# Sigmoid attention and a gated layer on one core: attention of all batches first, and the gated layer's products in 2x2x2 blocks with seven products in place of eight

## The chip, the core and the metric

The kernel runs on one core of a Trainium2 chip. Five engines work on their own instruction queues, each in order: TensorE (PE in the profile; its weight loads are PEld), VectorE (DVE), ScalarE (ACT), GpSimd (POOL) and SyncE (SP, which here only starts transfers). They wait for each other by semaphores. The metric is the device time of one execution in microseconds (us), the median of several runs; 675.48 us before the change. Where a reader sees "a product" below, it is a run of matmuls that sum into one PSUM bank.

## The reference, cut to what matters

```python
batch, n_heads, seq, head_dim = (4, 12, 448, 64)
d_model, d_ff = 768, 1536
scores = scale * np.matmul(q, k.transpose(0, 1, 3, 2)) - np.log(S)
attn = 1.0 / (1.0 + np.exp(-scores))            # a sigmoid, no sum over keys
attn_out = np.matmul(attn, v)
x = attn_out.transpose(0, 2, 1, 3).reshape(B * S, H * D)      # 1792 x 768
rms = np.sqrt(np.mean(x * x, axis=-1, keepdims=True) + 1e-06)
xn = x / rms * rms_g
g, val = xn @ w_gate, xn @ w_val                # 768 -> 1536, twice
out = (g * (1.0 / (1.0 + np.exp(-g))) * val) @ w_out          # 1536 -> 768
```

All in float32; the weights arrive as the bits of float64.

## The kernel before

A float32 operand of a product is held as two fp16 parts, hi and lo, and a product is hi·hi + hi·lo + lo·hi: three matmuls for each 128 rows of the contraction. A part is made by ScalarE (hi, a copy with a scale, `hi_of`) and VectorE (lo, `lo_of`). Weights are first put together as float32 from the two words of a float64 by three VectorE instructions on 768 columns (lines 349, 352, 353), then split.

Attention runs by pairs of heads, 24 pairs in all, six to a batch; a pair has four groups of keys (g = 0 to 3; the last, `MID`, has half the work). For each pair VectorE splits q and k (`qk_hi`, `qk_lo`, two pairs ahead), a transfer transposes them into T, VectorE swaps halves of T (`k_swap`, one pair ahead) and copies the shared slot of v (`v_mid`). `scores(i, g)` is four matmuls and a sigmoid on ScalarE; `av(i, g)` multiplies with v. For 13 of the pairs (`exact`: batches 0 and 1 and the last pair) the products with v are float32's own; for the other 11 the sigmoid's result and v are split, and the products are three fp16 matmuls.

The program is written out in order (`manual_schedule`). It takes two batches at a time: attention of batches 0 and 1, the gated layer of both for each slice of 128 columns of its weights (`ffn_in`, 18 matmuls of 448 columns for one batch and one of gate and value, 1728 in all), then the output layer of these two batches (`out_steps`) woven into the attention of batches 2 and 3, then the gated layer and the output layer of those. The gated layer's weights are so loaded and split twice, once for each two batches. In attention scores and products with v alternate group by group: scores of one group, then the product of the group `LAG` = 3 behind.

The rms norm of a batch (`norm`) is a list of parts: a matmul that sums squares over the features (`squares`), small VectorE steps (mean, guess, three Newton steps, `spread` to a diagonal), a matmul that spreads the factor to all rows (`rows`, called rinv in the profile), and six scalings with their hi and lo. The parts are drawn from the list `later`, with waits in between by the table `WAITS`.

Of the kernel before, what the change touches and what calls it, by code (L numbers as in the profile page):

```python
# [15 lines left out]
# Powers of two that keep both fp16 parts of a float32 operand in fp16's range.  # L16
SQ = 2.0**6
SA = 2.0**15
SX = 2.0**6
SW = 2.0**6  # L20
# [4 lines left out]
def attention_then_swiglu(  # L25
# [25 lines left out]
    NCC = DM // P  # L51
    NFC = DFF // P
    HALF = DM // 2
    NTOK = 2 * S // P
    TB = S // 4
# [3 lines left out]
    ld_p = ctx.enter_context(tc.tile_pool(name="ld", bufs=4))  # L59
    nat_p = ctx.enter_context(tc.tile_pool(name="nat", bufs=2))  # L60
    v_p = ctx.enter_context(tc.tile_pool(name="v", bufs=3))
    t_p = ctx.enter_context(tc.tile_pool(name="t", bufs=3))
    s_p = ctx.enter_context(tc.tile_pool(name="s", bufs=3))
    a_p = ctx.enter_context(tc.tile_pool(name="a", bufs=4))
    x_p = ctx.enter_context(tc.tile_pool(name="x", bufs=2))
    r_p = ctx.enter_context(tc.tile_pool(name="r", bufs=2))
    f_p = ctx.enter_context(tc.tile_pool(name="f", bufs=5))
    win_p = ctx.enter_context(tc.tile_pool(name="win", bufs=2))
    h_p = ctx.enter_context(tc.tile_pool(name="h", bufs=1))
    o_p = ctx.enter_context(tc.tile_pool(name="o", bufs=2))  # L70
# [11 lines left out]
    ATT = 0.82  # L82
    OUT_STEP = 4
    WARM = 20
    WAITS = ((9, 2, 1, 2, 1), (0, 1, 0, 1, 2), (8, 2, 0, 3, 3), (5, 2, 0, 4, 2))
# [5 lines left out]
    wo = const.tile([P, 2, NFC, DM], F16, name="wo")  # L91
    v3 = [const.tile([P, 2, 2 * D], F16, name=f"v3_{i}") for i in range(3)]
# [4 lines left out]
    def hi_of(engine, hi, f, scale):  # L97
        if engine is nc.scalar:
            nc.scalar.activation(hi, f, AF.Copy, scale=scale)  # L99
        else:  # L100
            nc.vector.tensor_scalar(hi, f, scale, None, ALU.mult)  # L101

    def lo_of(lo, f, hi, scale):
        nc.vector.scalar_tensor_tensor(lo, f, scale, hi, ALU.mult, ALU.subtract)  # L104

    lo_q = []

    def flush(keep):
# [4 lines left out]
    pairs = [(b, hp) for b in range(B) for hp in range(NPAIR)]  # L113
    ld, nat, vt, qkT, at, pav, xt, acc = ({} for _ in range(8))
# [5 lines left out]
    def load_qk(i, queue=nc.scalar):  # L120
        t = ld_p.tile([P, 2 * DM], F32, tag="ld", name="qkv")[:, : 3 * NSLOT * D]
        t = ld[i] = t.rearrange("p (t c d) -> p t c d", t=3, c=NSLOT)
        queue.dma_start(t[:, 0], rows_of(q, i, "(p c) d -> p c d"))  # L123
        queue.dma_start(t[:, 1], rows_of(k, i, "(c p) d -> p c d"))

    def load_v(i):
        vt[i] = v_p.tile([P, 2, NSLOT, D], F16, tag="nv", name="nv")
        if exact(i):
            vt[i] = vt[i].rearrange("p l c d -> p (l c d)").bitcast(F32).rearrange("p (c d) -> p c d", d=D)
        nc.sync.dma_start(vt[i] if exact(i) else ld[i][:, 2], rows_of(v, i, "(c p) d -> p c d"))  # L130

    # Parts of the rows of q and k: transposed they are [qh|ql] and [kh|kl], with [kl|kh] from the second;
    # a head's tokens are its queries in the order of every NSLOT-th one.
    def qk_hi(i):
        n = nat[i] = nat_p.tile([P, 2, NSLOT, 2, D], F16, tag="n", name="n")
        hi_of(nc.vector, n[:, :, :, 0], ld[i][:, 0:2], SQ)

    def qk_lo(i):
        n = nat[i]
        lo_of(n[:, :, :, 1], ld[i][:, 0:2], n[:, :, :, 0], SQ)  # L140

    def transpose(i):
        T = qkT[i] = t_p.tile([P, 3, NSLOT, P], F16, tag="T", name="T")
# [12 lines left out]

    def v_hi(i):
        if not exact(i):
            hi_of(nc.vector, vt[i][:, 0], ld[i][:, 2], SQ)

    def v_lo(i):
        if not exact(i):
            lo_of(vt[i][:, 1], ld[i][:, 2], vt[i][:, 0], SQ)

    def v_mid(i):
        """The slot that two heads share: once with either one's rows, over zeros."""
        for j in range(2):
            rows = slice(64 * j, 64 * j + 64)
            if exact(i):
                nc.vector.tensor_copy(v3[i % 3].bitcast(F32)[rows, j], vt[i][rows, MID])  # L170
            else:
                nc.vector.tensor_copy(v3[i % 3].rearrange("p j (l d) -> p j l d", l=2)[rows, j], vt[i][rows, :, MID])

    split_q = []

    def split_a(keep):
        while len(split_q) > keep:
            sg, a = split_q.pop(0)
            hi_of(nc.scalar, a[:, 0], sg, SA)
            lo_of(a[:, 1], sg, a[:, 0], SA)  # L180

    def scores(i, g):
        """Sigmoid of the scores, keys on partitions: 128 keys of either head, or 64 of each."""
        T = qkT[i]
        n = 1 if g == MID else 2
        ps = ps_s.tile([P, 2, 512], F32, tag="sc", name="sc")
# [20 lines left out]
        if g == MID:  # L207
            del qkT[i]
# [398 lines left out]
```

## Time and profile before

| | |
|---|---|
| median of 3 runs (lowest, highest) | 675.48 us (675.33, 676.51) |
| span of the profiled execution, first to last instruction | 672.7 us |
| PE busy in the span | 654.9 us, 97% |
| PE weight loads | 329.4 us, 49% |
| DVE busy | 420.7 us, 63% |
| ACT busy | 260.9 us, 39% |

The profile lists one execution, so its own time is the span and about 2.8 us that lie outside the first and last instruction, if it took as long as the median. A group of instructions is a line, an engine, an operation and a tile; "x36" counts them. In the views that go in order of time the first number is the start in us from the span's start, the second the length; a bracket at the end is the idle time of that engine just before, and what ended it. "PEclk" is the granted clock of TensorE as a share of 2.4 GHz; between its two levels, 1.00 and 0.50, a value is a mean over the stretch. A float32 matmul shows as two records.

### The profile page before, as it was taken

To read this page: it belongs to the slowest core of one execution; us is meant where nothing else is said; L and a number is where in the kernel's file an instruction comes from. 1 tells how busy PE (TensorE), PEld (TensorE's weight loads), DVE (VectorE), ACT (ScalarE), POOL (GpSimd) and SP (SyncE) were. 2 spreads that over 40 slices of the span, in tenths; PEclk is the share of its full clock that TensorE was granted. 3 is DMA by queue.
4 is the path that set the end of the run, shared out by engine and by line. 5 is a ranking of instruction groups with operands and counts; after the bars stand their busy time and mean duration, and the time that the engine had idled before them with its cause. 6 is when DMAs were issued, how large, how long until landed. Compare 5 with 4: busy or idle time off the path is not lost.

```text
span 672.7 us, 9121 instructions
## 1 busy us (share of the span) xinstructions
PE 654.9 (97%) x3672; PEld 329.4 (49%) x3672; DVE 420.7 (63%) x695; ACT 260.9 (39%) x392; POOL 0.7 (0%) x6
## 2 busy tenths in 40 slices
PE   7999999999999999999999999899999999999995
PEld 5233345555555554444454455355555555566663
DVE  4586786998888897778968637477576655100000
ACT  2666743333332335676766743123222222100000
POOL 0000000000000000000000000000000000000000
PEclk8999999999999999999999999899999999999998
DMA  9999730555455545788774002534323410011111
GB/s 195 237 251 208 198 107 1 188 189 188 147 188 183 187 130 110 174 135 175 144 145 85 25 22 89 182 111 154 111 94 120 128 36 0 1 32 34 33 35 33
DMA packets 134953, 80.80 MB, mean 120 GB/s; under 512 B 89856, under 2 KB 133376, under 8 KB 134912
## 3 DMA queue, kind: packets, MB, share of 16 engines
q1 hardware_dynamic: 115904, 71.97, 41.3%
q10 hardware_dynamic: 19008, 8.26, 5.3%
q8 instruction: 28, 0.46, 0.3%
q14 instruction: 13, 0.11, 0.0%
HBM read 63.70 MB, written 5.51 MB: 103 GB/s over the span
## 4 chain that ended last, share of the span: by engine, by line
PE 93%; DMA 4%; DVE 1%; ACT 0%; SPq 0%; issue 0%; ACTq 0%; DVEq 0%
PE h L368 47%; PE o L396 25%; PE av L226 10%; PE sc L195 10%; DMA T<-n 3%; DMA raw<-in_moe_w_val_dram 1%; DMA qkv<-in_k_dram 1%; PE ssq L262 1%; PE rinv L289 0%; DVE T L151 0%; ACT o L406 0%; DVE win L104 0%; DVE wf L353 0%; DVE wf L352 0%; SPq L123 0%
## 5 line engine op out<-in xcount | busy, mean ns | idle before, releaser
L368 PE MATMUL h<-x,win 128*128 128x448 f16 x1728 | 329.3, 354 | 2.8 <-DVE win L101 2.4
L368 PEld LDWEIGHTS <-win 128*128 128x128 f16 x1728 | 169.1, 98 | 162.5 <-DVE win L101 2.8
L396 PE MATMUL o<-wo,h 128*128 128x384 f16 x1008 | 170.3, 327 | 0.0
L396 PEld LDWEIGHTS <-h 128*128 128x128 f16 x1008 | 96.7, 98 | 72.2 <-issue 9.2
L195 PE MATMUL sc<-T 128*128 128x448 f16 (+1 forms) x384 | 81.9, 360 | 4.8 <-DMA T<-n 3.3
L99 ACT ACTIVATE win<-wf 128x768 f16<-128x768 f32 x40 | 33.7, 844 | 102.2 <-DVE wf L353 102.2
L382 DVE SCALAR_TENSOR_TENSOR hf<-h,hf 128x448 f32<-128x448 f32 x48 | 29.8, 620 | 52.5 <-PE h L368 52.5
L226 PE MATMUL av<-a,nv 128*64 128x448 f16 (+1 forms) x354 | 61.9, 446 | 0.0
L202 ACT ACTIVATE a<-sc,bias_s 128x896 f32<-128x896 f32 (+1 forms) x52 | 47.4, 915 | 31.6 <-PE sc L195 31.6
L195 PEld LDWEIGHTS <-T 128*128 128x128 f16 (+1 forms) x384 | 29.0, 102 | 61.7 <-issue 39.3
L353 DVE SCALAR_TENSOR_TENSOR wf<-raw,wf 128x768 uint32<-128x768 uint32 x56 | 53.6, 957 | 1.4
L104 DVE SCALAR_TENSOR_TENSOR win<-wf,win 128x768 f16<-128x768 f32 x48 | 45.9, 957 | 13.6 <-ACT win L99 13.4
L383 ACT ACTIVATE h<-hf 128x448 f16<-128x448 f32 x48 | 27.3, 570 | 67.8 <-DVE hf L382 67.8
L352 DVE SCALAR_TENSOR_TENSOR wf<-raw,wf 128x768 uint32<-128x768 uint32 x56 | 53.3, 952 | 0.1
L104 DVE SCALAR_TENSOR_TENSOR a<-sg,a 128x896 f16<-128x896 f32 (+1 forms) x44 | 42.8, 974 | 16.3 <-ACT a L99 15.8
L202 ACT ACTIVATE sg<-sc,bias_s 128x896 f32<-128x896 f32 (+1 forms) x44 | 40.0, 912 | 27.6 <-PE sc L195 21.0
L406 ACT ACTIVATE o<-o 128x384 f32<-128x384 f32 x28 | 13.7, 488 | 88.3 <-PE o L396 87.1
L99 ACT ACTIVATE a<-sg 128x896 f16<-128x896 f32 (+1 forms) x44 | 37.4, 850 | 0.0
L377 ACT ACTIVATE hf<-h 128x448 f32<-128x448 f32 x48 | 25.5, 531 | 23.2 <-PE h L368 23.2
L385 DVE TENSOR_TENSOR h<-hf,h 128x448 f16<-128x448 f32 x48 | 29.9, 622 | 6.9 <-ACT h L383 6.9
L349 DVE TENSOR_SCALAR wf<-raw 128x768 uint32<-128x768 uint32 x56 | 30.9, 553 | 3.7 <-DMA raw<-in_moe_w_val_dram 3.6
L104 DVE SCALAR_TENSOR_TENSOR n<-qkv,n 128x896 f16<-128x896 f32 x24 | 26.1, 1088 | 0.3
(50 smaller groups left out, 260.8 us busy)
## 6 DMA issues: line engine op xcount, KB each, us to landing
raw<-in_moe_w_gate_dram SPq DMA_DIRECT2D x22, 768.0 KB
raw<-in_moe_w_val_dram SPq DMA_DIRECT2D x22, 768.0 KB
raw<-in_moe_w_out_dram SPq DMA_DIRECT2D x12, 768.0 KB
out_dram<-o SPq DMA_DIRECT2D x24, 192.0 KB
qkv<-in_q_dram ACTq DMA_DIRECT2D x18, 224.0 KB
qkv<-in_k_dram ACTq DMA_DIRECT2D x18, 224.0 KB
nv<-in_v_dram SPq DMA_DIRECT2D x13, 224.0 KB
qkv<-in_v_dram SPq DMA_DIRECT2D x11, 224.0 KB
```

What stands on the lines that cost most here:

```text
L99: nc.scalar.activation(hi, f, AF.Copy, scale=scale)
L104: nc.vector.scalar_tensor_tensor(lo, f, scale, hi, ALU.mult, ALU.subtract)
L195: nc.tensor.matmul(o, m, r, start=(w == 0), stop=(w == 1))
L202: nc.scalar.activation(sg, ps[:, :n, :S], AF.Sigmoid, bias=bias_s, scale=1.0 / (math.sqrt(D) * SQ * SQ))
L226: nc.tensor.matmul(ps[64 * j : 64 * j + 64, :S], w, m, start=(g == 0 and n == 0), stop=(g == MID and n == len(parts) - 1),)
L349: lambda: nc.vector.tensor_scalar(b, r[:, :, 1], 3, 0x3FFFFFF8, ALU.logical_shift_left, ALU.bitwise_and),
L352: lambda: stt(b, r[:, :, 0], 29, b, ALU.logical_shift_right, ALU.bitwise_or),
L353: lambda: stt(b, r[:, :, 1], 0xC0000000, b, ALU.bitwise_and, ALU.bitwise_or),
L368: nc.tensor.matmul(ps[:, :S], w[:, g, l, c * P : c * P + P], xn(b, c, r), start=(c == 0 and n == 0), stop=(c == NCC - 1 and n == 2),)
L382: nc.vector.scalar_tensor_tensor(f, ps[:, :S], SH / (SX * SW), hold.pop(b), ALU.mult, ALU.mult)
L385: lambda: nc.vector.tensor_tensor(h[:, 1, fc, cols], f, h[:, 0, fc, cols], ALU.subtract)
L396: nc.tensor.matmul(ps[:, :HALF], h[:, l, c, t * P : t * P + P], wo[:, r, c, cols], start=(c == 0 and n == 0), stop=(c == NFC - 1 and n == 2),)
```

## The change

Attention of all four batches comes first, by the float32 products with v for all 24 pairs. Groups go by two: scores of two groups, then the products with v of the two groups before. The norms of batches 0, 1 and 2 and the splitting of the first two slices of the weights are drawn from `later` during attention, by a budget: each part has a cost, and a half step allows 0.72 (`SHARE`). `squares` now follows the last product of its batch where the list is empty.

Then comes the gated layer for all batches. Two batches (rows of x), two halves of the features and gate/value make a 2x2x2 block; `quad` computes such a block with seven products of half the contraction (9 matmuls each, 63 in all) where eight would be 72. For that the norm of the odd batch makes four sums and differences of x (1344 columns each), and `split_w` four of the weights (384 columns each); seven operands are split into hi and lo instead of four. Each slice of the weights is loaded and split once. The results are put together by VectorE: three additions of 448 columns, one of 896, two products and one lo of 896 to a quad. There are 24 quads of 63 matmuls, 1512.

The output layer comes last, for all batches; its first eight results are summed side by side in all eight PSUM banks, slice by slice of w_out, while the later slices are split. SBUF is divided by hand: buffers of attention, of the gated layer and of the output layer share the same places.

```diff
-    Two batches at a time: attention of their heads, the gated layer of both for each slice of
-    its weights, and the layer that follows together with the next two batches' attention."""
...
-    LAG = 3
-    W_FROM = (13, 17)
-    W_WAIT = 10
-    LATER_IN = 8
-    LATER_OUT = 5
...
-    WAITS = ((9, 2, 1, 2, 1), (0, 1, 0, 1, 2), (8, 2, 0, 3, 3), (5, 2, 0, 4, 2))
+    W_FROM = 40
+    SHARE = 0.72
...
+        def scale(k):
+            tt(x[:, k], x[:, k], ps[1][:, :S].unsqueeze(1).to_broadcast([P, NK, S]), ALU.mult)
+
+        def hi(slot, f):
+            nc.scalar.activation(xc[n, slot][:, 0], f, AF.Copy)
+
+        def lo(slot, f):
+            tt(xc[n, slot][:, 1], f, xc[n, slot][:, 0], ALU.subtract)
+
+        parts = [(squares, 0.2), (wait, 0.7), (mean, 0.2), (guess, 0.5)] + [(newton, 0.5)] * 3
+        parts += [(spread, 1.1), (rows, 0.2), (wait, 0.7)]
...
+        queue = [(s1, x[:, 0], x[:, 1], ALU.add, 3), (s2, s1, x0[:, 0], ALU.subtract, 4)]
+        queue += [(s4, x0[:, 1], s2, ALU.subtract, 6), (x[:, 0], x0[:, 0], x[:, 0], ALU.subtract, 5)]
...
+    def split_w(fc):
...
+        for o, f0, f1 in ((4, 2, 0), (2, 3, 2), (5, 3, 4), (6, 1, 5)):
+            first.append((lambda o=o, f0=f0, f1=f1: tt(wf[:, o], wf[:, f0], wf[:, f1], ALU.subtract), 0.6))
+
+        def hi(s):
+            nc.scalar.activation(t[:, 0, s], wf[:, s], AF.Copy, scale=SW)
+
+        def lo(s):
+            stt(t[:, 1, s], wf[:, s], SW, t[:, 0, s], ALU.mult, ALU.subtract)
+
+        cuts = [slice(0, 2), slice(2, 4), slice(4, 7)]
+        second.append((lambda: [hi(s) for s in cuts], 0.0))
+        second += [(lambda s=s: lo(s), 1.1) for s in cuts]
...
+    def quad(fc, n, fill):
+
+        y = y_b[(fc * NQ + n) % 2]
+        pa, pc = bank("ca"), banks("cc")
+        run_behind()
+        product(pa[:, :S], fc, n, 0, 0)
+        nc.scalar.activation(u_b, pa[:, :S], AF.Copy)
+        run_behind()
+        fill(0)
+        pb = bank("cb")
+        product(pb[:, :S], fc, n, 4, 5)
+        tt(u_b, u_b, pb[:, :S], ALU.add)
+        run_behind()
+        product(pc[:, 1, :S], fc, n, 5, 2)
+        tt(c_b, u_b, pc[:, 1, :S], ALU.add)
+        fill(1)
+        product(pc[:, 0, :S], fc, n, 3, 4)
+        tt(c_b, c_b, pc[:, 0, :S], ALU.add)
+        fill(2)
+        product(pa[:, :S], fc, n, 1, 1, True)
+        nc.scalar.activation(g_b, pa[:, :S], AF.Silu, scale=UNIT)
+        fill(3)
+        product(pc[:, 1, :S], fc, n, 2, 6, True)
+        fill(4)
+        product(pc[:, 0, :S], fc, n, 6, 3, True)
+
+        def sums():
+            tt(y, pc[:, :, :S], u_b.unsqueeze(1).to_broadcast([P, 2, S]), ALU.add)
+            nc.scalar.activation(y[:, 1], y[:, 1], AF.Silu, scale=UNIT)
...
+    def run_later(share):
+        credit[0] = min(credit[0] + share, 1.6)
+        while later and credit[0] > 0:
+            part, cost = later.pop(0)
+            part()
+            credit[0] -= cost
...
+        for n in range(0, len(todo) + 2, 2):
+            for i, g in todo[n : n + 2]:
+                scores(i, g)
+                for part in FILL[g]:
+                    part(i)
+                run_later(SHARE)
+            for i, g in todo[max(n - 2, 0) : n]:
+                av(i, g)
+                b, hp = pairs[i]
+                if hp == NPAIR - 1 and g == MID:
+                    later.extend(norm(b))
+                run_later(SHARE)
+            if n == W_FROM:
+                load_w(0)
+            if n == W_FROM + 16:
+                for fc in range(2):
+                    first, second = split_w(fc)
+                    later.extend(first + second)
...
+        for c in range(NFC):
+            for (t, e), ps in zip(first, pss):
+                out_part(ps, t, e, c)
+            if c + 3 < NFC:
+                if c + 6 < NFC:
+                    load_o(c + 6)
+                for x in sum(split_o(c + 3), []):
+                    x()
```

VectorE's queue during attention, one pair before the change while the first weights are split (`qkv`, `n`, `T`: q and k as loaded, split, transposed; `wf`, `win`: weights as float32 and split):

```order
L242 TENSOR_TENSOR acc<-acc,sq 128x448
L349 TENSOR_SCALAR wf<-h 128x768
L352 SCALAR_TENSOR_TENSOR wf<-h,wf 128x768
L101 TENSOR_SCALAR n<-qkv 128x14x64
L353 SCALAR_TENSOR_TENSOR wf<-h,wf 128x768
L101 TENSOR_SCALAR win<-wf 128x768
L104 SCALAR_TENSOR_TENSOR n<-qkv,n 128x14x64
L150 COPY T<-T 64x896
L151 COPY T<-T 64x896
```

The same queue now, at the pairs that the splitting of the first weights falls on (`xc` holds q, k and T there, `wr` the weights):

```order
L177 TENSOR_SCALAR xc<-xc 128x14x64
L328 SCALAR_TENSOR_TENSOR wr<-wr 128x768
L181 SCALAR_TENSOR_TENSOR xc<-xc 128x14x64
L191 COPY xc<-xc 64x896
L192 COPY xc<-xc 64x896
L355 TENSOR_TENSOR wr<-wr 128x384 x3
L198 COPY room<-room 64x64 x2
L355 TENSOR_TENSOR wr<-wr 128x384
L361 SCALAR_TENSOR_TENSOR wr<-wr 128x768 x2
L177 TENSOR_SCALAR xc<-xc 128x14x64
L361 SCALAR_TENSOR_TENSOR wr<-wr 128x1152
L181 SCALAR_TENSOR_TENSOR xc<-xc 128x14x64
```

Between one pair's `qk_lo` and `k_swap` and the next pair's stood at most one weight's splitting, with ten half steps of pause before each; now parts of the weights and of the norms stand there in every pair from the end of batch 1 to the last but one.

TensorE's queue at the first batch's sum of squares, before (`sc`, `av`, `ssq`: scores, products with v, sum of squares):

```order
L226 MATMUL av<-a,v_0_105 64x448 x2
L195 LDWEIGHTS T
L195 MATMUL sc<-T 64x448
...
L262 MATMUL ssq<-ones,acc 112x1 x4
L226 MATMUL av<-a,nv 64x448 x2
```

and now (`rinv`: the matmul that spreads the norm's factor):

```order
L252 MATMUL ssq<-ones,room 112x1 x4
L213 LDWEIGHTS xc
L213 MATMUL sc<-xc 128x448
...
L213 MATMUL sc<-xc 64x448
L227 MATMUL av<-room 64x448 x4
L279 MATMUL rinv<-room,ones 128x448
```

The sum of squares came one group of scores behind the batch's last product; it now comes right behind that product, and rinv two groups of scores and two of products later.

VectorE's queue in the gated layer, before, about one product of a gate and one of a value for one batch:

```order
L382 SCALAR_TENSOR_TENSOR hf<-h,hf 128x448
L349 TENSOR_SCALAR wf<-raw 128x768
L385 TENSOR_TENSOR h<-hf,h 128x448
L352 SCALAR_TENSOR_TENSOR wf<-raw,wf 128x768
L353 SCALAR_TENSOR_TENSOR wf<-raw,wf 128x768
L349 TENSOR_SCALAR wf<-raw 128x768
L104 SCALAR_TENSOR_TENSOR win<-wf,win 128x768
```

and now, one quad with the end of the quad before it (`cb`, `cc`: PSUM banks of the products):

```order
L355 TENSOR_TENSOR wr<-wr 128x384 x4
L418 TENSOR_TENSOR room<-cc,room 128x896
L422 SCALAR_TENSOR_TENSOR room<-room 128x448
L423 SCALAR_TENSOR_TENSOR room<-room 128x448
L402 TENSOR_TENSOR room<-room,cb 128x448
L427 TENSOR_TENSOR room<-room 128x896
L405 TENSOR_TENSOR room<-room,cc 128x448
L408 TENSOR_TENSOR room<-room,cc 128x448
L361 SCALAR_TENSOR_TENSOR wr<-wr 128x768 x2
L361 SCALAR_TENSOR_TENSOR wr<-wr 128x1152
```

What VectorE does for one result grew, and two of TensorE's seven products (lines 413 and 415, into `cc`) wait until it has read the bank that they add to (lines 405 and 408).

## Rows read from the trace of the kernel before

**Rows 1.** The page's first part: the span, and each engine's busy time, share and instructions.

```profile
span 672.7 us, 9121 instructions
PE 654.9 (97%) x3672; PEld 329.4 (49%) x3672; DVE 420.7 (63%) x695; ACT 260.9 (39%) x392; POOL 0.7 (0%) x6
```

**Rows 2.** Busy time of each engine by stage of the program: stretch, its length, then PE, PEld, DVE, ACT, POOL, granted clock, share of the DMA engines, GB/s. The stages: attention of batches 0 and 1, their gated layer, their output layer with attention of batches 2 and 3, the gated layer of these, and after the last output product.

```profile
11.20:94.00 82.80, 80.96 (x402) 27.27 (x403) 57.56 (x122) 57.03 (x79) 0.00 (x0) 0.98 1.01 217
94.00:260.40 166.40, 165.38 (x873) 85.13 (x871) 144.83 (x215) 53.00 (x86) 0.00 (x0) 1.00 0.47 147
260.40:414.60 154.20, 154.20 (x992) 76.75 (x991) 110.17 (x207) 98.01 (x140) 0.00 (x0) 1.00 0.53 107
414.60:583.00 168.40, 165.60 (x867) 84.86 (x866) 102.05 (x140) 44.14 (x72) 0.00 (x0) 0.99 0.31 100
665.00:672.70 7.70, 0.00 (x0) 0.00 (x0) 0.00 (x0) 0.40 (x1) 0.00 (x0) 0.64 0.09 29
```

**Rows 3.** The chain of work that ended last, followed back from the end: shares by engine.

```profile
PE 93%; DMA 4%; DVE 1%; ACT 0%; SPq 0%; issue 0%; ACTq 0%; DVEq 0%
```

**Rows 4.** The costliest group, the gated layer's matmuls, from the table of groups (count, busy us, mean ns of one record), and two pieces of the chain in order of time: the last output layer, and ScalarE's copy of its last result.

```profile
L368 PE MATMUL h<-x,win 128*128 128x448 f16 x1728 | 329.3, 354 | 2.8 <-DVE win L101 2.4
```
```profile
582.92 81.91 PE o L396 x504
...
664.91 0.49 ACT o L406
```

**Rows 5.** Pieces of the chain in attention of batches 0 and 1: a group's scores (four matmuls), a group's product with v (two matmuls, four records), the same place of the next pair, and the four last groups of products with v in a row.

```profile
42.74 0.86 PE sc L195 x4
43.60 0.90 PE av L226 x4
...
49.17 0.86 PE sc L195 x4
...
88.75 3.06 PE av L226 x16
```

**Rows 6.** TensorE in order of time in the same attention, one group of scores seen in two windows that end after its second and its fourth matmul.

```profile
57.29 0.55 PE L195 MATMUL sc<-T 128*128 128x448 f16 x2
```
```profile
57.29 0.93 PE L195 MATMUL sc<-T 128*128 128x448 f16 x4
```

**Rows 7.** The end of batch 1 and its norm in order of time: square on ScalarE, sum on VectorE, the sum of squares on TensorE (with TensorE's idle time before it in brackets), the first and the last of VectorE's small steps, and rinv.

```profile
91.83 0.54 ACT L239 ACTIVATE sq<-av 128x448 f32<-128x448 f32 x1 [1.86 <-PE av L226]
...
92.41 0.62 DVE L242 TENSOR_TENSOR acc<-acc,sq 128x448 f32<-128x448 f32 x1 [0.28 <-ACT sq L239]
...
93.09 0.95 PE L262 MATMUL ssq<-ones,acc 128*112 128x1 f32 x8 [1.33 <-DVE acc L242]
...
96.99 0.15 DVE L267 TENSOR_SCALAR m<-ssq 112x4 f32<-112x4 f32 x1
...
99.36 0.84 DVE L283 TENSOR_SCALAR diag<-ident,y 112x112 f32<-112x112 f32 x4
...
100.70 0.92 PE L289 MATMUL rinv<-diag,ones 112*128 112x448 f32 x2
```

**Rows 8.** VectorE's instructions by form from the table of groups (count | busy us, mean ns of one): joining of weights, splits and sums of 448, 768 and 896 columns, the swap and the copy of v's shared slot; and ScalarE's copy of 768 columns.

```profile
L353 DVE SCALAR_TENSOR_TENSOR wf<-raw,wf 128x768 uint32<-128x768 uint32 x56 | 53.6, 957 | 1.4
L349 DVE TENSOR_SCALAR wf<-raw 128x768 uint32<-128x768 uint32 x56 | 30.9, 553 | 3.7 <-DMA raw<-in_moe_w_val_dram 3.6
L385 DVE TENSOR_TENSOR h<-hf,h 128x448 f16<-128x448 f32 x48 | 29.9, 622 | 6.9 <-ACT h L383 6.9
L104 DVE SCALAR_TENSOR_TENSOR n<-qkv,n 128x896 f16<-128x896 f32 x24 | 26.1, 1088 | 0.3
L101 DVE TENSOR_SCALAR n<-qkv 128x896 f16<-128x896 f32 x24 | 15.0, 623 | 14.2 <-DMA qkv<-in_k_dram 14.1
L150 DVE COPY T<-T 64x896 f16<-64x896 f16 x24 | 9.3, 387 | 7.7 <-DMA T<-n 7.1
L170 DVE COPY v<-nv 64x64 f32<-64x64 f32 x26 | 4.9, 187 | 0.6
...
L99 ACT ACTIVATE win<-wf 128x768 f16<-128x768 f32 x40 | 33.7, 844 | 102.2 <-DVE wf L353 102.2
```

**Rows 9.** Two transfers as pieces of the chain: weights, 768 KB with other such loads beside them, and a pair's transpose.

```profile
415.95 8.16 DMA raw<-in_moe_w_val_dram
```
```profile
6.19 4.15 DMA T<-n
```

**Rows 10.** Four stretches as in rows 2: the busiest ten us of VectorE in attention, a stretch with TensorE's wait at batch 1's norm, and two with the longest idle times of TensorE; behind them, in order of time, the matmuls that ended these two idle times.

```profile
30.00:40.00 10.00, 9.99 (x49) 3.09 (x50) 9.66 (x17) 6.38 (x8) 0.00 (x0) 1.00 1.19 250
90.00:100.00 10.00, 8.67 (x51) 4.42 (x48) 9.13 (x26) 2.80 (x4) 0.00 (x0) 1.00 0.00 0
420.00:440.00 20.00, 17.20 (x83) 8.15 (x81) 8.66 (x13) 2.79 (x6) 0.00 (x0) 0.91 0.49 162
...
10.00:20.00 10.00, 9.15 (x37) 3.07 (x38) 5.95 (x12) 5.48 (x6) 0.00 (x0) 0.83 1.10 203
```
```profile
10.39 0.36 PE L195 MATMUL sc<-T 128*128 128x448 f16 x1 [2.77 <-DMA T<-n]
```
```profile
427.33 0.55 PE L368 MATMUL h<-x,win 128*128 128x448 f16 x2 [2.36 <-DVE win L101]
```

More of the change, by code (lines that the diff above doesn't have):

```diff
@@ new lines, in hi @@
+        def hi(slot, f):
[4 more added lines that the diff above has]
+        parts += [(spread, 1.1), (rows, 0.2), (wait, 0.7)]
+        if not odd:
+            for s in range(2):
+                parts += [
+                    (lambda s=s: scale(s), 1.6),
+                    (lambda s=s: hi(s, x[:, s]), 0.0),
+                    (wait, 0.7),
+                    (lambda s=s: lo(s, x[:, s]), 1.6),
+                ]
+            return parts
@@ L345, in split_w, with wait, to_f32 @@
+        return parts + [(wait, 0.7), (lambda a=behind: lo(*a), 1.6)]
+    def wait():
+        pass
+    def to_f32(f, r):
         b = f.bitcast(U32)
-        hi, lo = dest(u)
-        stt = nc.vector.scalar_tensor_tensor
         return [
@@ new lines, in attention_then_swiglu, with run_behind, product @@
+    PARTS = ((0, 0), (0, 1), (1, 0))
+    UNIT = 1.0 / (SX * SW)
+    behind = []
+    def run_behind():
+        if behind:
+            behind.pop(0)()
+    def product(ps, fc, n, a, b, more=False):
+        w = win[fc % 2]
+        for c in range(NK):
+            for m, (l, r) in enumerate(PARTS):
+                nc.tensor.matmul(
+                    ps,
+                    w[:, l, b, c],
+                    xc[n, a][:, r, c],
+                    start=(not more and c == 0 and m == 0),
+                    stop=(c == NK - 1 and m == 2),
+                    skip_group_check=more,
+                )
@@ new lines, in out_part, with out_end @@
+    def out_part(ps, t, e, c):
+        for n, (l, r) in enumerate(PARTS):
+            nc.tensor.matmul(
+                ps[:, :HALF],
+                h[c, t // NTOK][:, l, t % NTOK * P : t % NTOK * P + P],
+                wo[c][:, r, e * HALF : e * HALF + HALF],
+                start=(c == 0 and n == 0),
+                stop=(c == NFC - 1 and n == 2),
+            )
+    def out_end(ps, t, e):
+        cols = slice(e * HALF, e * HALF + HALF)
+        o = o_b[(2 * t + e) % 4]
+        nc.scalar.activation(o, ps[:, :HALF], AF.Copy, scale=1.0 / (SH * SO))
+        rows = out.rearrange("(b p c) d -> b c p d", b=B, c=NSLOT)
+        for j in range(2):
+            b, c = divmod(2 * t + j, NSLOT)
+            (nc.sync, nc.scalar)[j].dma_start(rows[b, c, :, cols], o[64 * j : 64 * j + 64])
@@ new lines, in attention_then_swiglu @@
+        first = [(t, e) for t in range(4) for e in range(2)]
+        pss = []
+        for _ in range(2):
+            both = banks("o2")
+            pss += [both[:, 0], both[:, 1]]
+        while behind:
+            run_behind()
+        pss += [bank("o") for _ in range(4)]
+        for c in range(NFC):
[6 more added lines that the diff above has]
+                    x()
@@ L580 @@
+        for (t, e), ps in zip(first, pss):
+            out_end(ps, t, e)
+        for t in range(4, NQ * NTOK):
+            for e in range(2):
+                ps = bank("o")
+                for c in range(NFC):
+                    out_part(ps, t, e, c)
+                out_end(ps, t, e)
 _INS = ["q", "k", "v", "moe_w_gate", "moe_w_val", "moe_w_out", "moe_rms_g"]
```

536 lines of the change are left out of this document (205 added, 331 removed).

## Prediction

> **What bounds the kernel now.** I read the page's busy times first: TensorE is busy for 654.9 of 672.7 us, VectorE for 420.7 [rows 1]. The chain of waits agrees, 93% of it is PE [rows 3]. An average says little of a change that moves whole stages, so the windows by stage come next: in each stage but the first and the last TensorE is busy for 98 to 100% and the clock is at 0.98 to 1.00 [rows 2]. Last, is TensorE really at its peak when it is busy? The gated layer's 1728 matmuls take 329.3 us, 190.6 ns each; 448 columns at the granted 2.4 GHz are 186.7 ns. The output layer's 504 take 81.91 us, 162.5 ns each [rows 4]. So the time is the count of matmuls, and it falls only if fewer are issued and no other engine takes TensorE's place. VectorE is the one to watch: at its busiest it works 9.66 of 10 us while TensorE still does 9.99 [rows 10].
>
> **What is removed.** 216 of 1728 gated matmuls: 216 x 0.1906 = 41.2 us. The second splitting of the weights goes too, but it lay on VectorE beside a full TensorE, so by itself it gives nothing.
>
> **What TensorE gets more of.** All pairs now take the float32 products with v. Such a pair takes 49.17 - 42.74 = 6.43 us with groups in alternation [rows 5]. A three-pass pair is bounded by the third stage: 154.2 us [rows 2], less 81.9 of output layer [rows 4], over 12 pairs: 6.0 (one of these pairs is exact already). So eleven pairs lose some 0.4 to 0.5 each, about 5 us. Groups by two give part back: a matmul of scores inside a run takes (0.93 - 0.55) / 2 = 0.19 us, so four take 0.76 [rows 6], against 0.86 between products with v; a group of products takes 3.06 / 4 = 0.765 in a run, 0.90 alone [rows 5]. If half of the switches go, a pair saves about 0.25 us: **6.17 us**.
>
> **What VectorE gets in attention.** A pair needs a split of q and k (0.623 + 1.088), two swaps (0.387 each), two copies (0.187 each) and one sum (0.622): 3.5 us [rows 8], far below 6.17. In batches 0 and 1 that stays so: norm 0 is four 1344-column instructions and small steps, spread over six pairs. From batch 1's sum of squares to the end of attention, 11.75 pairs, the order of VectorE's queue holds:
> - 9 splits, 10 pairs of swaps, 12 pairs of copies and 10 sums: 15.4 + 7.8 + 4.5 + 6.2 = 33.9 us;
> - two norms: small steps 3.2 each (96.99 to 100.20) [rows 7], and 15 instructions of 1344 columns. The trace has none so wide. From 448 to 896 columns the time goes from 0.622 to 1.088 [rows 8], 1.04 ns a column, so 1.56 us each as an estimate (the bound below is the 1.088 of 896, were the wide ones cheap): 6.4 + 23.4 = 29.8;
> - two splittings of weights: joining 2 x (0.553 + 2 x 0.957), four differences of 384 columns (0.55, by the same slope), two lo of 768 (0.957) and one of 1152 (1.36) [rows 8]: 10.4 each, 20.9 in all.
>
> That is **84.5 us on VectorE against 11.75 x 6.17 = 72.5, with the norms' matmuls 75 to 77, on TensorE**. VectorE becomes the bound of this half. It can't put the work off: the queue is in order, and the parts stand between one pair's split and the next pair's swap, without which that pair's scores don't start. I add 3 us for transposes queued on SP behind 1.5 MB of weights (8.16 us a load against 4.15 for a transpose [rows 9]; bounds 0 and 8), 0.4 for rinv, and 2.7 for the last pairs, where VectorE has little left and TensorE ends alone: 90.6.
>
> **The sum**, against the profiled execution (span 672.7; the 2.8 us outside it are kept):
> - start, unchanged: 11.2.
> - batches 0 and 1, now 80.6 us (11.21 to 91.8, the start of batch 1's last square [rows 2, 7]): twelve pairs save 3.0; two more groups of scores, 1.6; norm 0 adds 2.1, a wait of 1.3 for its sum as at batch 1 today [rows 7], since `squares` no longer has a group of scores ahead of it, and 0.8 for rinv, beside 0.95 and 0.92 that it costs today as well. 81.3, to 92.5.
> - batch 1's sum: wait 1.33 and 0.95 [rows 7]: 94.8.
> - batches 2 and 3, VectorE-bound: 90.6, to 185.4; batch 3's sum 0.95: 186.4.
> - gated layer: 1512 x 0.1906 = 288.2, and 5.6 in its first quads, where batch 3's norm (3.2 of small steps, then sums) is late and rinv takes 0.92: 480.2.
> - output layer, all batches: 1008 x 0.1625 = 163.8, and 2 for the last quad's sums, which must end before their PSUM banks are taken: 646.0. Its splitting of a slice (2.46 joining, 0.844 on ScalarE, 0.957 [rows 8]) runs three slices ahead.
> - tail 7.7 to 7.8 [rows 2]: 653.8.
>
> 653.8 against 672.7 is 18.9 less; with 2.8 outside, **656.6, say 657 us**. Of the 41.2 us, 22.3 are given back, 18 of them in the half that VectorE bounds (90.6 - 72.5).
>
> **Why the gated layer costs nothing more.** A quad lasts 63 x 0.1906 = 12.0 us on TensorE. For two quads VectorE has 10.4 of weights and 2 x (5 x 0.622 for 448 columns + 2 x 1.088 for 896 [rows 8] = 5.3) for the results, 21.0 together against 24.0, 88%. The places that can stall are the sixth and seventh product (lines 413 and 415), which add to a bank that VectorE must have read. By the order it has read them at 6.2 and 7.8 us into the quad; TensorE comes there at 8.6 and 10.3. Cover is 2.4 us, and a part of the weights (at most 1.36) in the way leaves over 1 us of it. If that cover were gone, a wait would cost its length 24 times.
>
> **Rivals.**
> *B, the backlog is hidden:* wide VectorE instructions nearer the lower bound (15 x 0.47 = 7 us less) and TensorE stays the bound in attention: 13 us less, 644. For: 9.66 busy and no wait [rows 10]. Against: the slope in rows 8, and the sum must fall by over 8 us. 0.07.
> *G, the quads stall:* the PSUM banks come 0.5 us late in every quad, 24 x 0.5 = 12: 669. For: VectorE at 88%, in order, with waits on ScalarE's copies between. Against: the cover above. It is slower than before only from 0.77 us a quad. 0.13.
> *C, slower, by the clock:* in the VectorE-bound half TensorE waits for about 1.5 us in a mean pair (90.6 / 11.75 = 7.7, less 6.17), and for 3.5 in one with four wide instructions (3.5 + 4 x 1.56 = 9.7). Rows 10 have the clock at 0.83 in the ten us of an idle time of 2.77 and at 0.91 in the twenty of one of 2.36; after 1.33 us it stays at 1.00. A pair wholly at the lower level, 1.2 GHz, would take 12.3 us instead of 7.7, 4.6 more: from four of the twelve pairs the saving of 18 is gone, and with seven the time is 656.6 + 32, about 689. Against: what a low clock takes comes out of the idle time first. One drop as in 420 to 440 costs 0.09 x 20 = 1.8 us of TensorE's work, and 6.17 + 1.8 = 8.0 is only 0.3 above the mean pair; then TensorE has no idle time and the clock rises again, as it did behind both waits. 0.10.
> The Trainium skill ("TensorE: Matmul & The Clock Gate", section "HAM oscillation — how this bites in real kernels") says that a wait in each iteration can throw the clock back at each of them, so that the price is paid per iteration and not once; by that rule the time would be rival C's. Rows 10 agree that a single wait does it; no row of the kernel before shows it repeated.
> The change does do what it says: 63 matmuls a quad are in the order. What remains, 0.04, is a mixture of G and small waits, 674 to 677, no change.
>
> **How the numbers follow.** Forecast 652 to 667 (transposes 0 to 8, norm and wide instructions by their bounds): 0.66. B 0.07, G 0.13, C 0.10, the rest 0.04. 0.2%, 1.35 us, is about what a measurement can tell from no change. Faster: 0.66 + 0.07 + most of G = 0.84; within 0.2%: 0.05; slower: C and a remainder of G, 0.11. The range goes from 647, which leaves out most of B, to 672, which takes in most of G: what is outside is C, B, the rest and a little of G, 0.2.
>
> **What would show it.** Attention ends at about 186 us; from 95 to 183 VectorE is busy for over 95% and TensorE for about 80%, with its waits before scores, ended by `k_swap` on VectorE. 24 quads at 12.0 us, with no idle time before lines 413 and 415. Output layer 166 us, tail 7.8. Wrong: a granted clock well under 1.00 from 95 to 185 (C), idle times in each quad (G), or TensorE near 100% in that half (B).

## The result and the profile after

The changed kernel takes **684.27 us** (median of 4 runs, 682.68 to 685.66) against 675.4 of the kernel before: a ratio of 1.014, with a 95% interval of 1.0112 to 1.0169. It is slower, where 657 was forecast. The profiled execution has a span of 680.9 us.

The page's first part, for the span and the busy times [rows 1], and the chain's shares by engine [rows 3]:

```profile
span 680.9 us, 8362 instructions
PE 625.7 (92%) x3368; PEld 314.8 (46%) x3368; DVE 412.1 (61%) x639; ACT 242.5 (36%) x332; POOL 0.7 (0%) x6
```
```profile
PE 54%; DVE 33%; issue 5%; ACT 4%; DMA 2%; ACTq 0%; SPq 0%; DVEq 0%
```

TensorE's busy time did fall, by 29.2 us. But the span left over grew from 18 to 55 us, and a third of the chain, 1% before, now runs through VectorE. Where, the windows by stage tell (columns as in [rows 2]); the stages are attention of batches 0 and 1, of 2 and 3, the gated layer, the output layer, and what follows its last product:

```profile
11.20:92.00 80.80, 78.28 (x401) 29.23 (x401) 49.60 (x104) 56.91 (x74) 0.00 (x0) 0.98 1.00 197
92.00:190.30 98.30, 82.30 (x409) 31.36 (x406) 80.31 (x150) 66.21 (x86) 0.00 (x0) 0.95 0.69 146
190.30:509.10 318.80, 293.36 (x1517) 148.88 (x1517) 243.01 (x334) 95.25 (x133) 0.00 (x0) 0.98 0.18 57
509.10:676.90 167.80, 164.43 (x1009) 98.50 (x1007) 34.33 (x41) 22.40 (x39) 0.00 (x0) 1.00 0.21 65
676.90:680.90 4.00, 0.00 (x0) 0.00 (x0) 0.00 (x0) 0.46 (x1) 0.00 (x0) 1.00 0.19 49
```

| stretch | forecast, us | profiled, us | difference |
|---|---|---|---|
| start to batch 1's sum of squares | to 93.85 | to 93.86 | 0.0 |
| from there to the first quad | 92.55 | 96.4 | +3.9 |
| gated layer | 293.8 | 318.8 | +25.0 |
| output layer | 165.8 | 167.8 | +2.0 |
| tail | 7.8 | 4.0 | -3.8 |

The sum is 27.1, which is 680.9 less the forecast 653.8. The gated layer is the miss: of its 25.0 us, some 20 lie in the last 22 of the 24 quads and 4.8 in the first two. TensorE is busy for 293.36 us in it, and 25.4 us are idle time. (That 293.36 is close to the 293.8 forecast for the whole stage is chance: the forecast had 288.2 of gated matmuls and 5.6 of the first quads.) The table of groups says before what, for the products into `cc`:

```profile
L382 PE MATMUL cc<-xc,wr 128*128 128x448 f16 x864 | 176.8, 355 | 25.4 <-DVE room L405 25.4
```

And the instructions of one quad in order of time (idle time of the engine in brackets) say which product: the second of the two groups of nine into `cc` here is the quad's fourth product, line 407:

```profile
421.27 1.87 PE L382 MATMUL cc<-xc,wr 128*128 128x448 f16 x9
...
421.54 0.62 DVE L402 TENSOR_TENSOR room<-room,cb 128x448 f32<-128x448 f32 x1 [0.99 <-ACT room L424]
422.07 1.08 DVE L427 TENSOR_TENSOR room<-room 128x896 f16<-128x896 f32 x1
423.17 0.62 DVE L405 TENSOR_TENSOR room<-room,cc 128x448 f32<-128x448 f32 x1
423.84 1.86 PE L382 MATMUL cc<-xc,wr 128*128 128x448 f16 x9 [0.71 <-DVE room L405]
```

The third product runs into one bank of the pair; line 405 reads that bank when it ends; the fourth product goes into the other bank and yet starts only when line 405 is done. TensorE stands idle for 0.71 us here and for 0.86 to 0.93 in every other quad: 16.6 us in 21 quads. The second quad, behind batch 3's norm, waits for 6.70 us and the last for 2.11; only the first has no wait, since rinv stands there between the third and the fourth product.

```profile
502.28 1.86 PE L382 MATMUL cc<-xc,wr 128*128 128x448 f16 x9 [2.11 <-DVE room L405]
```

### The profile page after: what moved, and what is told of

Same layout as the page of the kernel before. It is cut to its first block, busy times and chain, and to the rows that moved or that the text cites. A ratio compares the mean times of both kernels' runs of the same rounds, so it can differ in the third digit from the quotient of the medians.

```text
span 680.9 us, 8362 instructions
## 1 busy us (share of the span) xinstructions
PE 625.7 (92%) x3368; PEld 314.8 (46%) x3368; DVE 412.1 (61%) x639; ACT 242.5 (36%) x332; POOL 0.7 (0%) x6
## 3 DMA queue, kind: packets, MB, share of 16 engines
q1 hardware_dynamic: 92400, 48.97, 29.2%
## 4 chain that ended last, share of the span: by engine, by line
PE 54%; DVE 33%; issue 5%; ACT 4%; DMA 2%; ACTq 0%; SPq 0%; DVEq 0%
PE o L449 24%; PE cc L382 13%; PE av L227 6%; PE sc L213 6%; PE ca L382 4%; DVE room L418 4%; DVE wr L355 3%; DVE wr L327 3%; DVE room L405 2%; DVE room L402 2%; DVE room L422 2%; DMA xc<-xc 2%; DVE wr L328 2%; DVE wr L324 2%; DVE room L423 2%
## 5 line engine op out<-in xcount | busy, mean ns | idle before, releaser
L382 PEld LDWEIGHTS <-wr 128*128 128x128 f16 x1512 | 148.5, 98 | 169.6 <-issue 35.3
L382 PE MATMUL cc<-xc,wr 128*128 128x448 f16 x864 | 176.8, 355 | 25.4 <-DVE room L405 25.4
L449 PE MATMUL o<-xc,room 128*128 128x384 f16 x798 | 133.3, 326 | 3.3 <-ACT room L460 2.4
L449 PEld LDWEIGHTS <-room 128*128 128x128 f16 x798 | 78.1, 98 | 55.2 <-issue 3.7
L215 ACT ACTIVATE room<-sc,bias_s 128x896 f32<-128x896 f32 x96 | 84.3, 916 | 48.0 <-PE sc L213 46.6
L213 PE MATMUL sc<-xc 128*128 128x448 f16 (+1 forms) x384 | 78.4, 364 | 12.3 <-ACT room L215 6.9
L227 PE MATMUL av<-room 128*64 128x448 f32 x384 | 84.3, 559 | 0.0
L460 ACT ACTIVATE room<-o 128x384 f32<-128x384 f32 x28 | 13.7, 491 | 111.3 <-PE o L449 107.5
L382 PE MATMUL ca<-xc,wr 128*128 128x448 f16 x216 | 46.0, 359 | 0.0
L382 PE MATMUL cb<-xc,wr 128*128 128x448 f16 x216 | 44.8, 352 | 0.0
L327 DVE SCALAR_TENSOR_TENSOR wr<-wr 128x768 uint32<-128x768 uint32 x31 | 29.7, 959 | 1.0
L328 DVE SCALAR_TENSOR_TENSOR wr<-wr 128x768 uint32<-128x768 uint32 x31 | 29.6, 955 | 0.6
```

The costliest lines, as they stand in the source:

```text
L213: nc.tensor.matmul(o, m, r, start=(w == 0), stop=(w == 1))
L215: nc.scalar.activation(a[:, :n], ps[:, :n, :S], AF.Sigmoid, bias=bias_s, scale=1.0 / (math.sqrt(D) * SQ * SQ))
L227: nc.tensor.matmul(ps[64 * j : 64 * j + 64, :S], w, a[:, 0 if g == MID else j], start=(g == 0), stop=(g == MID))
L327: lambda: stt(b, r[:, :, 0], 29, b, ALU.logical_shift_right, ALU.bitwise_or),
L328: lambda: stt(b, r[:, :, 1], 0xC0000000, b, ALU.bitwise_and, ALU.bitwise_or),
L382: nc.tensor.matmul(ps, w[:, l, b, c], xc[n, a][:, r, c], start=(not more and c == 0 and m == 0), stop=(c == NK - 1 and m == 2), skip_group ...
```

## The experiments

Theory 1: the wait before the fourth product is a dependency that the order of the code and the pair of banks make, a round trip from TensorE to VectorE and back; it is there however idle VectorE is. Rival 2: VectorE's queue is too full. Rival 3: the fourth product needs line 405's result. The other runs ask about the half of attention that came out 3.9 us over.

**e1: line 405 behind the fourth product.**

```diff
-        tt(c_b, u_b, pc[:, 1, :S], ALU.add)
         fill(1)
         product(pc[:, 0, :S], fc, n, 3, 4)
+        tt(c_b, u_b, pc[:, 1, :S], ALU.add)
```

> Edit: in a quad the addition that reads the first bank of the pair (line 405) is issued behind the fourth product instead of ahead of it; nothing else changes. Theory 1: the 25.4 us that TensorE stood before the fourth product come from a wait for line 405, which only reads the other bank of the pair; without it 22 steady quads lose 0.86 us each (25.74 us for two quads becomes 24.0 to 24.2) and the time falls by 17 to 21, to 663 to 667. Rival 2, VectorE's queue is too full in the gated layer: the wait moves to the sixth product and the time falls by under 6, to 678 or more.

664.76 us (660.09 to 665.61), 0.9844 of the kernel before (0.9803 to 0.9885). The same group's row in its table of groups:

```profile
L382 PE MATMUL cc<-xc,wr 128*128 128x448 f16 x864 | 174.2, 356 | 5.5 <-DVE room L408 5.5
```

```profile
221.77 6.28 PE L382 MATMUL cc<-xc,wr 128*128 128x448 f16 x18 [5.49 <-DVE room L408]
```

Of 25.4 us, 5.5 are left, all in one wait, that of the sixth product of the second quad, behind batch 3's norm (line 408 is here the read of the fourth product's bank). One line moved turns the change from slower than before into faster. Rival 2 is out.

**e2: the two banks as two buffers**, the order kept.

```diff
-        pa, pc = bank("ca"), banks("cc")
+        pa = bank("ca")
...
+        p1, p0 = bank("cc"), bank("cd")
...
-            tt(y, pc[:, :, :S], u_b.unsqueeze(1).to_broadcast([P, 2, S]), ALU.add)
+            tt(y[:, 1], p1[:, :S], u_b, ALU.add)
+            tt(y[:, 0], p0[:, :S], u_b, ALU.add)
```

> Edit: the order stays (line 405 ahead of the fourth product), but the two banks are two buffers instead of one pair; the sum of 896 columns at a quad's end becomes two of 448 (about 0.16 us more on VectorE). Theory 1, in its form that the wait comes from the pair being one buffer: no wait before the fourth product, two quads in 24.0 to 24.2 us, 663 to 668. Rival 3, the fourth product needs line 405 in itself: two quads stay at 25.7, about 684. Rival 2 (VectorE's queue): 678 or more.

In one execution: 659.21 us. In several:

> The kernel of e2 again, timed: its one look gave 659.2 us with no wait ahead of the fourth product. Theory 1 expects 657 to 663, faster than before by 1.5 to 2.5%; should the look have been a lucky one, it is like e1 (664.8).

**657.33 us** (656.71 to 661.39), 0.9739 (0.9712 to 0.9766). Two groups of e2_timed (by the lines of its own kernel: L406 is the changed kernel's line 405), and in order of time the third and fourth product (`cc`, `cd`) of one quad and the third of the quad two further on:

```profile
L382 PE MATMUL cd<-xc,wr 128*128 128x448 f16 x432 | 89.6, 352 | 0.1
L382 PE MATMUL cc<-xc,wr 128*128 128x448 f16 x432 | 89.5, 352 | 3.1 <-DVE room L419 1.7 <-DVE room L406 1.5
```
```profile
228.84 1.87 PE L382 MATMUL cc<-xc,wr 128*128 128x448 f16 x9
230.54 1.86 PE L382 MATMUL cd<-xc,wr 128*128 128x448 f16 x9
...
252.68 1.87 PE L382 MATMUL cc<-xc,wr 128*128 128x448 f16 x9
```

The fourth product follows the third without a gap although line 405 stands ahead of it, and two quads take 252.68 - 228.84 = 23.84 us. So it doesn't need line 405: it waited because the two banks were one buffer, and in this program a write to one half waits for a read of the other. Rival 3 is out. (e2 also takes the two banks from another pool; e1, which leaves buffer and pool as they are, loses the same wait.) VectorE does slightly more here than before the edit, and only the second quad still stalls: its third product for 1.67 us and its sixth for 1.46, the 3.1 in the row.

**e5: VectorE half empty, the order as in the changed kernel.**

```diff
-                parts = list(split[to][0])
+                parts = []
...
-                parts = list(split[fc + 1][1])
+                parts = []
```

> Leaves out part of the computation: in the gated layer slices 2 to 11 of the weights are neither loaded nor split, so VectorE has 10.4 of its 21.0 us for two quads less; the order of the rest is that of the changed kernel. Theory 1: the wait before the fourth product is a round trip (third product ends, line 405, fourth product starts) and stays at 0.7 to 0.9 us in each quad, two quads in 25.4 to 25.8 us, 676 to 684 (a part of the first quads' delay may go). Rival 2: with VectorE half empty the wait goes, two quads in 24.0, 660 to 665.

685.14 us in one execution. The group's row, and two of TensorE's waits in order of time:

```profile
L382 PE MATMUL cc<-xc,wr 128*128 128x448 f16 x864 | 176.8, 355 | 23.8 <-DVE room L405 23.8
```
```profile
233.59 1.86 PE L382 MATMUL cc<-xc,wr 128*128 128x448 f16 x9 [0.71 <-DVE room L405]
246.38 1.86 PE L382 MATMUL cc<-xc,wr 128*128 128x448 f16 x9 [0.71 <-DVE room L405]
```

0.71 us in 21 quads (6.69 in the second and 2.11 in the last, as in the changed kernel) and two quads in 25.6 (2 x 12.79): with half of VectorE's work gone the wait is what it was. Theory 1 holds; VectorE's other work made only the 0.16 by which each second quad's wait was longer.

**e8: attention without the weights.**

```diff
+    nc.gpsimd.memset(w_room[:, 2 * RW + FW :], 0.0)
...
-            if n == W_FROM:
-                load_w(0)
-            if n == W_FROM + 16:
-                for fc in range(2):
-                    first, second = split_w(fc)
-                    later.extend(first + second)
+            if n == 80:
+                load_w(2)
```

> Leaves out part of the computation: the changed kernel, with the first two slices of the weights neither loaded nor split (zeros stand in their place), so in the second half of attention VectorE has 20.9 us less and SP no weights to load. By the prediction's sum (VectorE-bound: 84.5 against 75 to 77) the stretch from batch 1's to batch 3's sum of squares, 95.6 us in the changed kernel, falls to 78 to 83. If it stays over 90, VectorE's sum was not the bound, and waits of single steps were.

675.33 us in one execution. Windows from batch 1's to batch 3's sum of squares, of the changed kernel and of e8:

```profile
93.80:189.40 95.60, 80.94 (x396) 30.52 (x396) 78.91 (x148) 64.89 (x83) 0.00 (x0) 0.95 0.69 146
```
```profile
94.80:181.00 86.20, 77.57 (x396) 29.29 (x396) 60.48 (x122) 59.74 (x77) 0.00 (x0) 0.98 0.68 139
```

18.4 us of VectorE's work give 9.4 us of time: less than the forecast 13 to 18, more than the bound for "VectorE was not it". (The five traces with this attention unedited, of the changed kernel, e1, both runs of e2 and e5, have 95.6 to 99.2 us here, so 9.4 is against the shortest.) Over the whole stretch VectorE was busy for 78.9 of 95.6 us, but that is a mean. The changed kernel in five windows, VectorE's busy time third:

```profile
92.00:110.00 18.00, 15.44 (x82) 5.97 (x78) 15.30 (x36) 12.12 (x17) 0.00 (x0) 1.00 0.78 162
110.00:130.00 20.00, 17.56 (x85) 6.29 (x84) 19.63 (x28) 14.99 (x19) 0.00 (x0) 0.91 0.66 136
130.00:150.00 20.00, 17.25 (x88) 6.37 (x88) 19.06 (x32) 15.06 (x21) 0.00 (x0) 1.00 1.04 235
150.00:170.00 20.00, 13.39 (x60) 5.51 (x56) 17.69 (x42) 8.92 (x12) 0.00 (x0) 0.83 0.80 168
170.00:190.00 20.00, 18.37 (x100) 6.91 (x96) 8.63 (x15) 15.12 (x21) 0.00 (x0) 1.00 0.18 35
```

From 110 to 150 VectorE is full, at 97%, with TensorE at 87%, much as the prediction had it; from 170 on VectorE has little left and TensorE, at 92%, works off what it is behind with. The bound changes inside the stage. Three of TensorE's waits there:

```profile
93.86 0.95 PE L252 MATMUL ssq<-ones,room 128*112 128x1 f32 x8 [1.33 <-DVE room L235]
...
114.26 2.51 PE L213 MATMUL sc<-xc 128*128 128x448 f16 x8 [2.18 <-ACT room L215]
...
164.49 1.86 PE L279 MATMUL rinv<-room,ones 112*128 112x448 f32 x2 [4.25 <-DVE room L273]
```

**e3, e6, e7: the weights earlier.** Each puts other lines in the place of those that e8 takes out of the loop; e3 on the changed kernel (first load at 2, slices split from 10 and from 36), e6 and e7 on e2. Shown is e6; e7 has 56 in the place of 42:

```diff
+            if n == 12:
+                load_w(0)
+            if n in (22, 42):
+                first, second = split_w((22, 42).index(n))
+                later.extend(first + second)
```

> Edit: the first two slices of the weights are loaded and split earlier, the first from half step 10 (batch 0), the second from 36 (batch 1) instead of from 56 (batch 2): 20.9 us of VectorE leave the half of attention that it bounds. Theory 1: attention ended at 190.4; from 92 on TensorE has 72.5 of pairs and some 6 of norms' matmuls and waits, VectorE 64, so it ends at 174 to 181 and the time falls by 10 to 16, to 668 to 674. Rival: transfers in batch 0 (DMA share already 1.09) come late and batch 0 takes back 5 us or more of it; or the clock drops anyway and less than 6 are gained.

> Edit on the kernel of e2: the weights' first load at half step 12, the first slice split from 22, the second from 42, so that batches 2 and 3 have 20.9 us of VectorE's work less and the loads miss the crowded first 30 us. If the half of attention behind batch 1 is bound by VectorE and e3 lost its gain to the early loads alone, it falls from 95 to 101 us to some 83 to 87 and no more than 5 us come back in batch 1 (whose VectorE then has 41 us for 37): 649 to 655. If the loads or the queue in batch 1 take it back, 657 to 665.

> Edit on the kernel of e2: only the first slice is early (load at 12, split from 22), the second stays at 56: 10.4 us leave the VectorE-bound half, 74 against 75 to 77 of TensorE. VectorE-bound: the half falls by 7 to 10 us, 650 to 655. If it is not VectorE's sum but single waits (sum of squares, rinv, transposes) that make the half long, it falls by under 4: 656 to 661.

e3: 690.12 us, 1.0236 (1.0194 to 1.0277). The rival's side. The half behind batch 1's sum fell from 95.6 to 85.3 us (107.52 to 192.83), as theory 1 said, but the sum came 13.7 us later. Waits of e3 up to 110 us (us in total, times, longest), a piece of its chain, its window from 30 to 50 us, and TensorE in order of time:

```profile
DVE xc L177 <- DMA xc<-in_k_dram: 10.6, 2, 7.7
```
```profile
20.26 11.37 DMA xc<-xc
```
```profile
30.00:50.00 20.00, 14.89 (x78) 5.43 (x75) 17.93 (x33) 13.56 (x18) 0.00 (x0) 0.99 1.10 237
```
```profile
49.31 2.71 PE L213 MATMUL sc<-xc 128*128 128x448 f16 x8 [4.58 <-ACT room L215]
...
107.52 0.95 PE L252 MATMUL ssq<-ones,room 128*112 128x1 f32 x8 [1.33 <-DVE room L235]
...
192.83 0.95 PE L252 MATMUL ssq<-ones,room 128*112 128x1 f32 x8 [1.33 <-DVE room L235]
```

The transfers that the rival names have a part, but not the whole. A transpose issued behind the weights' loads landed after 11.37 us (median 4.4), and VectorE, in order, stood for k for 7.7 us at one time; up to there TensorE had lost about 4 us against the changed kernel. Its longest wait, 4.58 us, came 20 us later, when VectorE had been busy for 17.93 of 20 us with the splitting, now in batch 0. The wait for k alone doesn't explain it: the changed kernel's VectorE waits for k for 14.5 us in the same stretch, at most 4.4 at a time.

e6: **653.50 us** (650.76 to 655.24), 0.9684 (0.9645 to 0.9722), the fastest of all, and faster than both kernels. Its sums of squares of batches 1 and 3:

```profile
100.50 1.65 PE L252 MATMUL ssq<-ones,room 128*112 128x1 f32 x8 [3.60 <-DVE room L235]
...
184.39 1.02 PE L252 MATMUL ssq<-ones,room 128*112 128x1 f32 x8 [1.33 <-DVE room L235]
```

83.9 us, where e2_timed has 99.2; some 5 come back ahead of it. By the medians 3.8 us are gained on e2, and each of e6's four runs is below each of e2's five; the two profiled executions lie at opposite ends of their kernels' runs and show more. e7: 657.94 us (0.9748), no different from e2; its half took 93.2 us, 6.0 less, and the sum of batch 1 came 4.6 later. Its time lies in the range of the single waits, the fall of its half between the two ranges: it doesn't tell the two accounts apart.

**e9, e10: the single waits in attention.** On e2 and on e6:

```diff
-        parts = [(squares, 0.2), (wait, 0.7), (mean, 0.2), ...
+        parts = [(wait, 1.7), (squares, 0.2), (wait, 0.7), (mean, 0.2), ...
...
-            parts += [(lambda o=o, slot=slot: hi(slot, o), 0.0)]
             parts += [(lambda a=behind: lo(*a), 1.6)]
+            parts += [(lambda o=o, slot=slot: hi(slot, o), 0.0)]
```

> Edit on the kernel of e2: a pause ahead of squares, so that the sum of squares stands behind a group of scores instead of right behind its batch's last product, and in the odd norms ScalarE's copy of a sum (hi) is issued one VectorE step later, so that the sigmoids behind it don't stand with it. e8 left 86 us between the sums of squares of batches 1 and 3 with VectorE relieved, of which the waits before sums, rinv and scores are 8.6. If these single waits add to the time by themselves, 3 to 6 us go: 651 to 655. If VectorE's sum bounds this half anyway (20.9 us of splitting still in it), TensorE waits as long elsewhere: 656 to 660.

> The same edit on the kernel of e6 (splitting moved ahead, VectorE no longer the bound behind batch 1). Both accounts expect a gain here, 3 to 7 us of the single waits: 646 to 651. None (652 to 656) would say that the waits are only the places where a full VectorE shows.

660.64 us (0.9803, 0.9775 to 0.9831) and 661.30 (0.981, 0.9781 to 0.984). e9 gained nothing, as VectorE's side said, but it missed that range as well: it is 0.6 us above it and slower than e2. e10 is a miss of both accounts, 8 us slower than e6. TensorE's waits in order of time, of e9 and of e10:

```profile
93.61 0.95 PE L252 MATMUL ssq<-ones,room 128*112 128x1 f32 x8 [0.87 <-DVE room L235]
...
139.88 2.49 PE L213 MATMUL sc<-xc 128*128 128x448 f16 x8 [3.37 <-ACT room L215]
...
160.36 2.50 PE L213 MATMUL sc<-xc 128*128 128x448 f16 x8 [3.37 <-ACT room L215]
```
```profile
66.05 1.65 PE L213 MATMUL sc<-xc 128*128 128x448 f16 x4 [4.81 <-ACT room L215]
...
110.61 1.65 PE L213 MATMUL sc<-xc 128*128 128x448 f16 x4 [4.00 <-ACT room L215]
```

The waits that were aimed at got shorter (before batch 1's sum 0.87 us in e9 for 2.33 in e2_timed, none in e10 for 3.60 in e6) and others of 3 to 5 us came elsewhere, before scores. That what is issued later lands on another pair would explain it; no run shows it. e10's loss lies in attention: its first quad starts at 194.68 us, e6's at 185.28.

## Why the prediction was wrong

**The step that failed** is "The places that can stall are the sixth and seventh product (lines 413 and 415)". Those two never stalled in the changed kernel. The fourth did, in 23 of 24 quads, for 25.4 us in all. The working asked which product adds to a bank that VectorE must have read, and counted VectorE's time to get there; it didn't ask which product writes to the *buffer* that VectorE is reading. The pair is one buffer, line 405 stands ahead of the fourth product in the code, so the order of this wait could be read from the code; that it goes by the buffer and not by the bank no row had shown before e1 and e2. Cover of 2.4 us was right for the two places named (2.6 in the steady quads of e2_timed: line 405's read ends at 231.36 us, the sixth product starts at 233.95) and said nothing of this one, where it is zero by construction: VectorE can start line 405 only when the third product ends.

**Rival G** had the right stage, and its price per quad, 0.5 us, was too low: with e2's 23.84 for two quads against 25.74 (nine pairs of quads from 230.85 to 462.52), the dependency costs 0.95 us a quad, above its threshold of 0.77. Its mechanism, a full VectorE in order, was not the cause (e5).

**What held.** The count: 216 matmuls less are 41 us less, and without the wait the gated layer takes 292.3 us (195.3 to 487.6 in e2_timed) for 293.8 forecast:

```profile
195.30:487.60 292.30, 289.03 (x1517) 148.93 (x1517) 245.98 (x356) 94.98 (x133) 0.00 (x0) 0.99 0.19 63
```

The first half of attention with its exact products and groups by two came to 93.86 for 93.85 forecast (94.3 to 95.9 in the four other traces with this attention unedited); the wide instructions to 1.55 us for 1.56. With the one wait away the kernel takes 657.33 us, and 657 was forecast. That this fits to 1 us is luck: in e2_timed's profiled execution, the slowest of its five, attention to the first quad is 9 us longer than forecast, the output layer 2 longer, and the gated layer 1.6 and the tail 3.7 shorter. Why the tail is shorter no run shows.

**A term mis-sized: the half behind batch 1's sum,** 92.55 forecast, 96.4 measured, and still more in e2_timed (99.9, from 95.4 to 195.3). Moving VectorE's work away pays (e6, e8), so its work does bound a part of this half. (Both edits move the weights' loads as well; that these alone would pay was not run apart.) The trace of the changed kernel shows how the terms came out between the sums of batches 1 and 3. The instructions that the prediction counted as 84.5 us last 84.2 in sum, but many start up to 0.1 us before the one ahead of them ends, and VectorE's busy time is 78.9. Its idle time is 16.7 us where 6.1 was put down: waits for transposes under 1 (3 forecast; 4.7 in e2_timed), for the norms' sums and rinv 3.1 (0.4 for rinv), and 10.3 in three waits for the last pairs' squares, behind 170 us (2.7 for the last pairs). So the mis-sized term is the last pairs, where VectorE was done and TensorE, behind from its waits before, ended alone. Of TensorE's own waits those before scores that `k_swap` ended, the predicted sign, were only 2.6 us; sigmoids on ScalarE ended 5.7, rinv 5.1 (4.25 of it at one time) and sums 2.7. What a single one of these waits costs stays open, since e9 and e10 moved waits and did not remove them; so does why e10 lost 8 us to e6.

**The quad that the norm of batch 3 reaches** also cost more: to the third quad's start 34.4 us for the 29.6 forecast, but 30.0 in e2_timed, so most of the excess was the pair again. TensorE waited 6.70 us, and the nine matmuls behind the wait took 3.52 us, where nine take 1.86 at the full clock; the granted clock had fallen:

```profile
215.03 3.52 PE L382 MATMUL cc<-xc,wr 128*128 128x448 f16 x9 [6.70 <-DVE room L405]
218.34 3.06 PE L382 MATMUL ca<-xc,wr 128*128 128x448 f16 x9
```

**Rival C** did not come about as a price paid per pair: the granted clock from 92 to 190 was 0.95 in the mean. That is the place of "HAM oscillation — how this bites in real kernels" in "TensorE: Matmul & The Clock Gate" of the Trainium skill: by that rule a wait in each round can throw the clock back each time. The trace agrees in part: in the windows of e8's section it fell behind some waits (0.91 from 110 to 130 us, 0.83 from 150 to 170) and not behind others (1.00 from 130 to 150), and 0.95 over 98 us is, as an estimate, some 5 us of TensorE's work, not 32.

## What to carry to other kernels

When a product is split into several that meet in PSUM, look for each at what is issued just ahead of it that reads *any part of the same buffer*: a read of the other half is a full round trip, 0.95 us each time here, of which 0.62 is the read itself, and a VectorE with half the work left shortened it by no more than 0.16. Give each bank its own buffer, or issue the read behind the next product; then count cover. And a stage's sum of busy time says who can bound it, not how long it takes: here VectorE was full for 40 us, while TensorE waited, and short of work in the last 20, while TensorE caught up, so look at slices of a stage and not at its mean.

## What the runs showed of the hardware

The same wait in the same place cost the clock in one execution and not in another. Windows from 50 to 60 us, and TensorE's wait in them, of the changed kernel and of e1, which are the same program up to there:

```profile
50.00:60.00 10.00, 8.67 (x40) 3.57 (x40) 6.62 (x24) 3.85 (x6) 0.00 (x0) 0.83 0.57 98
```
```profile
51.57 0.95 PE L252 MATMUL ssq<-ones,room 128*112 128x1 f32 x8 [1.33 <-DVE room L235]
```
```profile
50.00:60.00 10.00, 7.78 (x44) 3.27 (x42) 7.72 (x27) 4.42 (x7) 0.00 (x0) 1.00 0.56 116
```
```profile
52.82 0.95 PE L252 MATMUL ssq<-ones,room 128*112 128x1 f32 x8 [1.33 <-DVE room L235]
```

1.33 us idle and then 0.95 of one-column matmuls: the clock was at 0.83 over the ten us in one and at 1.00 in the other, as it was at batch 1's norm before the change [rows 10]. In the first the eight records of products with v that start at 53.74 us took 3.21 us, in the second, from 54.88, 1.67. The length of a wait alone doesn't tell whether the clock falls.
